# Other fillers in TensorE's program: inside the line of the first products and, new, between the quarter products

## The chip, the cores and the metric

The kernel runs on one core of one Trainium2 chip. The metric is the device time of one execution in microseconds, lower is better; a profiled execution also has a span, from the first to the last instruction that the profile shows.

## The reference

A retention layer (8 batches, 8 heads, 576 positions, head size 64) is followed by a feed-forward layer on the joined heads.

```python
def _attn_ref(q, k, v):
    B, H, S, D_ = q.shape                      # 8, 8, 576, 64
    scores = np.matmul(q, k.transpose(0, 1, 3, 2)) / np.sqrt(D_)
    gamma = 1.0 - 2.0 ** (-5.0 - np.arange(H, dtype=np.float32))
    rel = np.arange(S)[:, None] - np.arange(S)[None, :]
    Dmat = np.where(rel >= 0, gamma[:, None, None] ** rel[None, :, :], 0.0)
    return np.matmul(scores * Dmat[None], v)
# x: (4608, 512), the heads of a token side by side
h = x @ w_in                                   # (512, 2048)
out = (h * np.cos(h)) @ w_out                  # (2048, 512)
```

## The kernel before

The 4608 tokens are cut into nine tiles of 512 (`n` = 0 to 8), and for the attention into 18 blocks of 256, two to a tile. The attention is done in chunks with a running state: `turned` transposes queries and keys, `sums_of` makes the states, `scores` the masked scores, `out_own` and `out_carried` the outputs. All of these are 64x64 matmuls, each on a quarter of the array; the text calls them quarter matmuls. Each takes a weight load and a matmul, so two rows of TensorE's program.

The feed-forward layer of a tile has two parts. `mm1` makes `h` (line 525): from tile 2 on, eight blocks of eight matmuls of 512 columns. ScalarE takes the cosine of a block and VectorE multiplies, and the PSUM bank is then free. The second product is done by `mm2_seven` as seven products of half-size blocks (Strassen's scheme), in the order 1, 2, 6, 4, 7, 5, 3; `product` (line 608) issues each of them as 16 matmuls of 256 columns (line 640). In tiles 3 to 6, product 2 is preceded by transposes, product 4 and product 3 by one `visit` each: a unit of 120 or 128 quarter matmuls that gives one block's outputs and the next block's states and scores. So the order of TensorE's work in such a tile is: 64 matmuls of line 525; product 1; transposes; products 2 and 6; first unit; products 4, 7, 5; second unit; product 3. The order is written out by hand, and every engine runs its program in order.

TensorE's program holds fillers besides. `addr_align(2, k)` puts a row that does nothing where the next row's address, counted in rows, isn't k modulo 2; since weight load and matmul are two rows, calls with k in turn 1, 0, 1, 0 give one row each. In the trace such a row is a NOP of line 508. `spread` (line 500, called at line 533 after each matmul of line 525) puts `fillers[n]` of them evenly between the matmuls of tile n's first product:

```python
    fillers = {0: 96, 1: 80, 2: 80, 3: 126, 4: 48, 5: 64, 6: 64, 7: 128}
```

`product` has none.

Of the kernel before, what the change touches and what calls it, by code (L numbers as in the profile page):

```python
# [17 lines left out]
def kernel(  # L18
# [21 lines left out]
    DG = DM // P  # L40
    ET = DF // P
# [3 lines left out]
    W = 512  # L45
# [44 lines left out]
    w_in_sb = consts.tile([P, DG, DF], BF16)  # L90
    w_out_sb = consts.tile([P, ET, DM], BF16)

    fillers = {0: 96, 1: 80, 2: 80, 3: 126, 4: 48, 5: 64, 6: 64, 7: 128}
    tiles = {}

    class Chunk:
# [400 lines left out]
        for run in rest:  # L497
            run()

    def spread(n, w):  # L500

        want = fillers.get(n, 0)
        done = tiles["g", n, "done"]
        whole = ET * DG * W
        if want and not done:
            nc.tensor.addr_align(2, 0)
        for u in range(done * want // whole, (done + w) * want // whole):
            nc.tensor.addr_align(2, 1 - u % 2)
        tiles["g", n, "done"] = done + w

    def mm1(n, et, c0, w, bank, inside={}):
        if ("g", n) not in tiles:
            tiles["g", n] = gp.tile([P, ET, W], BF16, tag="gT", name="gT")
            tiles["g", n, "done"] = 0
        gT, xT = tiles["g", n], tiles["x", n]
        m = 1024 // w
        ps = psum.tile([P, m, w], F32, tag=bank, name="h")
        steps = [(j, dg) for j in range(m) for dg in range(DG)]
        in_parts = (n, et, c0) in ((0, 0, 0), (0, 4, 0))
        if in_parts:  # L520
            steps.sort(key=lambda u: u[1] // 2)
        for u, (j, dg) in enumerate(steps):
            if u % DG == 0 and u // DG in inside:
                inside[u // DG]()
            nc.tensor.matmul(  # L525
                ps[:, j, :],
                lhsT=w_in_sb[:, dg, (et + j) * P : (et + j + 1) * P],
                rhs=xT[:, dg, c0 : c0 + w],
                start=dg == 0 and not (in_parts and w < 512 and j % 2),
                stop=dg == DG - 1,  # L530
                skip_group_check=in_parts,
            )
            spread(n, w)
        if m in inside:
            inside[m]()

        cosh = cosp.tile([P, m, w], F32, tag="cosh", name="cosh")
        nc.scalar.activation(cosh, ps, ACTF.Sin, bias=half_pi, scale=1.0)  # L538
        nc.vector.tensor_mul(gT[:, et : et + m, c0 : c0 + w], ps, cosh)  # L539
# [3 lines left out]
    def w_quarter(r, c):  # L543
        return w_out_sb[:, r * E2 : (r + 1) * E2, c * N2 : (c + 1) * N2]
# [63 lines left out]
    def product(n, x, early=None):  # L608
        gT = tiles["g", n]
        parts = [(j, 0, N2) for j in range(2)]  # L610
        fold = n in (1, last)
        fresh = x not in ((6, 7, 3) if fold else (6, 7))
        if fresh:
            tag = {1: "n", 2: "st", 4: "m" if n == 1 else "st", 5: "st", 3: "n"}[x]
            if x == 5 and n == last:
                tiles["o", x] = [
                    psum.tile([P, c], F32, tag=t, name="o")
                    for t, c in (("b", N2), ("m", N2 // 2), ("a", N2 // 2))
                ]
            else:  # L620
                ps = psum.tile([P, 2, N2], F32, tag=tag, name="o")
                tiles["o", x] = [ps[:, j] for j in range(2)]
                tiles["all", x] = ps
        if x in (5, 3) and n == last:
            parts = [(0, 0, N2), (1, 0, N2 // 2), (1, N2 // 2, N2)]
        dst = tiles["o", x if fresh else 5 if x == 3 else 1]
        lhs = {1: gT[:, :E2, :256], 2: gT[:, E2:, :256], 4: gT[:, E2:, 256:]}.get(x)
        if lhs is None:
            lhs = tiles["gs", n, x]
        rhs = {1: w_quarter(0, 0), 2: w_quarter(1, 0), 3: w_quarter(1, 1)}.get(x)  # L630
        if rhs is None:
            rhs = w_sum[x]
        order = [(e, i) for e in range(E2) for i in range(len(parts))]
        if len(parts) > 2:
            order.sort(key=lambda u: u[1])
        for u, (e, i) in enumerate(order):
            if early and u == len(order) // 4:
                early()
            j, c0, c1 = parts[i]
            nc.tensor.matmul(  # L640
                dst[i],
                lhsT=lhs[:, e, j * P : (j + 1) * P],
                rhs=rhs[:, e, c0:c1],
                start=(fresh and e == 0 and (i == 0 or len(parts) > 2)),
                stop=(e == E2 - 1 and (i == len(parts) - 1 or len(parts) > 2)),
                skip_group_check=True,
            )
        return parts

    def stored_rows(r0, c0, c1, t, queues=(nc.sync, nc.sync)):  # L650
# [7 lines left out]
    def mm2_seven(n, at, stored, xs=(1, 2, 6, 4, 7, 5, 3), early=None):  # L658
# [26 lines left out]
        for x in xs:  # L685
# [8 lines left out]
            if x == 6 and n > 1:  # L694
                late_sums(n, (3,))
            parts = product(n, x, early)
            if x == 1:
                c11 = copied("a", 1)
# [256 lines left out]
    for n in range(NT):  # L955
# [37 lines left out]
        if n == 0:  # L993
# [24 lines left out]
            order = [(t, e) for e in range(part) for t in range(4)]  # L1018
# [3 lines left out]
            for done, (t, e) in enumerate(order):  # L1022
# [9 lines left out]
                for u in range(2 * (t == 1) if t < 2 else 1) if e == ET - 1 else ():  # L1032
                    u = u if t < 2 else t
# [119 lines left out]
```

## Time and profile before

| what | us |
|---|---|
| median of 3 runs | 293.08 |
| lowest and highest | 292.98 to 293.34 |
| the profiled execution | 292.63 |
| its span | 290.9 |
| line 525, tile 4: 64 matmuls, 48 fillers | 13.81 |
| line 525, tile 7: 64 matmuls, 128 fillers | 13.81 |
| products 4, 7 and 5 of a tile, 48 matmuls | 5.34 |
| a unit of quarter matmuls, tiles 3 to 7 | 1.27 to 1.36 |

The span is what lies between the first and the last instruction; 1.7 us of the profiled execution lie around it. PE is TensorE's matmuls, PEld its weight loads, DVE VectorE, ACT ScalarE, POOL GpSimd, SP SyncE; PEldq marks a row that TensorE's sequencer runs by itself, without the array. A matmul's record lasts longer than the distance to the next, so paces are taken from the distance of starts. The times of the table's last four rows are distances between the start of the first matmul of the part and that of the next part.

### The profile page before, as it was taken

The numbers are of one execution on the slowest core, as the hardware profiler recorded it, in microseconds if no ns is written. First come the engines' busy times: TensorE is split into PE (matmuls) and PEld (weight loads), VectorE is DVE, ScalarE is ACT, GpSimd is POOL, SyncE is SP. The second block draws the span as 40 slices with busy tenths as digits, with TensorE's granted clock in tenths as the row PEclk, the third lists the DMA queues.
The fourth block names the chain that finished last, engine by engine and source line by source line (L and its number), as shares of the span: only waits on it lengthen the run. The fifth ranks groups of instructions, "written<-read, shape, count | busy, mean of one in ns | idle before, by whom it ended". The sixth has DMA issues, their size and how long they took to land.

```text
span 290.9 us, 10529 instructions
## 1 busy us (share of the span) xinstructions
PE 284.3 (98%) x4336; PEld 191.3 (66%) x4336; DVE 218.5 (75%) x309; ACT 170.7 (59%) x200; POOL 147.9 (51%) x169
## 2 busy tenths in 40 slices
PE   7999999999999999999999999999999999999994
PEld 2664446888854786478647874687458845884584
DVE  5767758999967967896789677977698669745943
ACT  6756216756677655676467746673767476536620
POOL 7840435698977993379136923593348024002400
PEclk9999999999999999999999999999999999999999
DMA  7999999997997989837690589139101220122013
GB/s 218 275 171 205 252 235 247 224 220 195 223 224 183 268 207 230 210 78 176 170 227 15 129 200 217 42 99 231 38 0 41 65 49 0 41 51 59 0 38 108
DMA packets 103853, 42.62 MB, mean 146 GB/s; under 512 B 68480, under 2 KB 103296, under 8 KB 103808
## 3 DMA queue, kind: packets, MB, share of 16 engines
q1 hardware_dynamic: 99104, 37.37, 52.5%
q0 software_dynamic: 4256, 4.19, 9.1%
q8 instruction: 36, 0.59, 0.8%
q10 hardware_dynamic: 448, 0.39, 0.4%
q14 instruction: 9, 0.07, 0.1%
HBM read 36.70 MB, written 9.44 MB: 159 GB/s over the span
## 4 chain that ended last, share of the span: by engine, by line
PE 94%; DVE 3%; DMA 1%; issue 0%; ACT 0%; DVEq 0%; ACTq 0%
PE h L525 43%; PE o L640 34%; PE o L1025 5%; PE ov L449 3%; PE tr L239 3%; PE ov L477 2%; PE sc L332 2%; DVE ret L312 1%; PE st L365 1%; DMA fk<-in_k_dram 1%; DVE qks L171 1%; PE sc L299 0%; PE tr L260 0%; ACT ot L670 0%; PE idle L270 0%
## 5 line engine op out<-in xcount | busy, mean ns | idle before, releaser
L525 PE MATMUL h<-xT,w_in_sb 128*128 128x512 bf16 (+1 forms) x656 | 127.4, 353 | 0.0
L539 DVE TENSOR_TENSOR gT<-h,cosh 128x1024 bf16<-128x1024 f32 x72 | 87.8, 1221 | 27.3 <-ACT cosh L538 26.8
L538 ACT ACTIVATE cosh<-h,half_pi 128x1024 f32<-128x1024 f32 x72 | 80.2, 1115 | 40.7 <-PE h L525 40.7
L525 PEld LDWEIGHTS <-w_in_sb 128*128 128x128 bf16 x656 | 63.5, 98 | 58.6 <-DMA w_in_sb<-in_moe_w_in_dram 0.2
L579 POOL TENSOR_TENSOR gs<-gT 128x512 bf16<-128x512 bf16 x30 | 38.1, 1271 | 99.6 <-DVE gT L539 99.0
L640 PEld LDWEIGHTS <-gs 128*128 128x128 bf16 x528 | 49.6, 98 | 5.9
L203 POOL TENSOR_TENSOR qks<-fk,gkc 128x512 bf16<-128x512 f32 x32 | 39.0, 1237 | 5.1 <-DMA fk<-in_k_dram 5.1
L640 PEld LDWEIGHTS <-gT 128*128 128x128 bf16 x384 | 36.6, 98 | 6.1
L666 DVE TENSOR_TENSOR ot<-ot,o 128x512 f32<-128x512 f32 x35 | 23.3, 683 | 20.2 <-ACT ot L670 12.6
L245 ACT COPY qkT<-tr 128x1024 bf16<-128x1024 bf16 x29 | 27.7, 1021 | 12.0 <-PE tr L239 11.0
L203 POOL TENSOR_TENSOR qks<-fq,gq 128x512 bf16<-128x512 f32 x28 | 31.2, 1134 | 4.6 <-DMA fq<-in_q_dram 4.6
L640 PE MATMUL o<-w_out_sb,gs 128*128 128x256 bf16 (+1 forms) x264 | 30.7, 270 | 0.0
L640 PE MATMUL o<-w_out_sb,gT 128*128 128x256 bf16 x256 | 30.6, 273 | 0.0
L640 PE MATMUL o<-ws,gs 128*128 128x256 bf16 (+1 forms) x264 | 30.4, 269 | 0.0
L670 ACT COPY ot<-o 128x512 f32<-128x512 f32 x33 | 19.2, 586 | 18.1 <-PE o L640 17.5
L341 DVE TENSOR_TENSOR ret<-sc,mask_c 128x512 bf16<-128x512 f32 x32 | 20.6, 683 | 7.5 <-PE sc L332 6.6
L214 POOL CAST vb<-fv 128x512 bf16<-128x512 f32 x35 | 22.0, 650 | 6.7 <-DMA fv<-in_v_dram 6.7
L425 ACT CAST sb<-s_all 128x768 bf16<-128x768 f32 (+2 forms) x17 | 15.6, 919 | 14.0 <-DVE s_all L416 13.9
L416 DVE TENSOR_TENSOR s_all<-st,s_all 128x256 f32<-128x256 f32 x49 | 20.7, 422 | 1.9 <-PE st L365 0.6
L496 ACT CAST xT<-ov 128x1024 bf16<-128x1024 f32 x16 | 16.2, 1012 | 9.6 <-PE ov L477 9.4
L579 DVE TENSOR_TENSOR gs<-gT 128x512 bf16<-128x512 bf16 (+1 forms) x24 | 15.8, 660 | 0.6
L579 DVE TENSOR_TENSOR gs<-gs,gT 128x1024 bf16<-128x1024 bf16 x16 | 15.2, 948 | 0.3
(83 smaller groups left out, 213.7 us busy)
## 6 DMA issues: line engine op xcount, KB each, us to landing
out_dram<-ot SPq DMA_DIRECT2D x68, 128.0 KB, 2.7
fk<-in_k_dram SPq DMA_DIRECT2D x28, 256.0 KB, 5.3
fv<-in_v_dram SPq DMA_DIRECT2D x28, 256.0 KB, 4.8
fq<-in_q_dram SPq DMA_DIRECT2D x12, 512.0 KB, 5.0
w_out_sb<-in_moe_w_out_dram POOLq DMA_DIRECT2D x4, 512.0 KB, 9.6
fq<-in_q_dram SPq DMA_DIRECT2D x4, 384.0 KB, 7.3
fk<-in_k_dram SPq DMA_DIRECT2D x2, 512.0 KB, 5.0
fv<-in_v_dram SPq DMA_DIRECT2D x2, 512.0 KB, 5.9
```

The lines of the kernel that those rows point to most:

```text
L203: return eng.tensor_tensor(out=dst.rearrange("p b a d -> p a b d"), in0=src.rearrange("p (a b) d -> p a b d", a=2), in1=by.rearrange("p (a ...
L214: runs[y](vb[:, y], f[:, :, y, :] if j < NP_B else f[:, y])
L245: lambda r=r: evacs[r](tiles["qkT", j][:, :, :, :, r * HP : r * HP + HP], pss[r])
L341: nc.vector.tensor_tensor(out=ret[:, he].rearrange("p b y i -> p (b y) i"), in0=ps[he].rearrange("p b y i -> p (b y) i"), in1=mask_c.unsqu ...
L416: nc.vector.tensor_tensor(out=s32[:, u], in0=ps[c.half][:, c.y], in1=s32[:, u - 1] if u else tiles["run"], op=ALU.add,)
L525: nc.tensor.matmul(ps[:, j, :], lhsT=w_in_sb[:, dg, (et + j) * P : (et + j + 1) * P], rhs=xT[:, dg, c0 : c0 + w], start=dg == 0 and not (i ...
L538: nc.scalar.activation(cosh, ps, ACTF.Sin, bias=half_pi, scale=1.0)
L539: nc.vector.tensor_mul(gT[:, et : et + m, c0 : c0 + w], ps, cosh)
L579: i = eng.tensor_tensor(out=tiles["gs", n, x][:, e : e + step], in0=a[:, e : e + step], in1=b[:, e : e + step], op=op_,)
L640: nc.tensor.matmul(dst[i], lhsT=lhs[:, e, j * P : (j + 1) * P], rhs=rhs[:, e, c0:c1], start=(fresh and e == 0 and (i == 0 or len(parts) > 2)),
L666: return lambda: nc.vector.tensor_tensor(out=out_, in0=in0, in1=in1, op=ALU.add)
L670: held.append(lambda ps=tiles["all", x]: nc.scalar.copy(t, ps))
```

## The change

The numbers of fillers in `mm1` become others for tiles 2 to 7. The padding itself moves into a helper, `filled`, which `product` calls too: after each of the 48 matmuls of products 4, 7 and 5 in tiles 3 to 6 it puts its share of `between[n]` fillers, 160 or 176 to a tile, so three or four to a matmul. The total of fillers goes from 686 to 950 in `mm1`, and from none to 688 in the products. Nothing else is changed.

```diff
-    fillers = {0: 96, 1: 80, 2: 80, 3: 126, 4: 48, 5: 64, 6: 64, 7: 128}
+    fillers = {0: 96, 1: 80, 2: 31, 3: 103, 4: 144, 5: 144, 6: 144, 7: 208}
+    between = {3: 160, 4: 176, 5: 176, 6: 176}
...
-    def spread(n, w):
-
-        want = fillers.get(n, 0)
-        done = tiles["g", n, "done"]
-        whole = ET * DG * W
+    def filled(want, done, w, whole):
+
         if want and not done:
             nc.tensor.addr_align(2, 0)
         for u in range(done * want // whole, (done + w) * want // whole):
             nc.tensor.addr_align(2, 1 - u % 2)
+
+    def spread(n, w):
+
+        done = tiles["g", n, "done"]
+        filled(fillers.get(n, 0), done, w, ET * DG * W)
         tiles["g", n, "done"] = done + w
...
             nc.tensor.matmul(
                 dst[i],
...
                 stop=(e == E2 - 1 and (i == len(parts) - 1 or len(parts) > 2)),
                 skip_group_check=True,
             )
+            if x in (4, 7, 5):
+                filled(between.get(n, 0), (4, 7, 5).index(x) * len(order) + u, 1, 3 * len(order))
         return parts
```

## The prediction

> **What bounds the kernel now.** I read the page first, then what TensorE waits for, then the chain of waits around one tile's products, then the records of the filler line, and last the granted clock in a stretch where TensorE is only partly busy.
>
> ```profile
> PE 284.3 (98%) x4336; PEld 191.3 (66%) x4336; DVE 218.5 (75%) x309; ACT 170.7 (59%) x200; POOL 147.9 (51%) x169
> ...
> q8 instruction: 36, 0.59, 0.8%
> ...
> PE 94%; DVE 3%; DMA 1%; issue 0%; ACT 0%; DVEq 0%; ACTq 0%
> ```
>
> TensorE is busy 98% of the span and is 94% of the chain that ended last. Queue q8 brings 36 packets of 16 KB; the trace has 9369 rows of TensorE's program (4336 weight loads, 4336 matmuls, 685 fillers, 12 others), so one packet is 256 rows of 64 bytes: these are the blocks that the change speaks of. TensorE's own waits, as the waits view gives them:
>
> ```profile
> PE idle L270 <- DVE zeros L814: 1.3, 1, 1.3
> PE ov L449 <- DVE ret L312: 0.5, 2, 0.3
> ```
>
> Both lie at the start. From tile 3 on TensorE waits for nobody, so anything that slows it goes into the end one for one. The chain, in order of time, through tile 3's products (start, length, what):
>
> ```profile
> 132.07 0.25 PE ov L449 x16
> 132.32 0.26 PE st L365 x32
> 132.57 0.29 PE sc L332 x32
> 132.87 0.27 PE ov L449 x15
> 133.13 0.29 PE ov L477 x31
> 133.43 5.34 PE o L640 x48
> 138.77 0.25 PE ov L449 x16
> ```
>
> The five pieces before 133.43 are one stretch of quarter matmuls, 256 rows in 1.36 us; 138.77 begins the next. Between them stand the 48 matmuls of products 4, 7 and 5, in 5.34 us, 111 ns each, and no row of another kind. Here the change puts 160 fillers (tile 3) or 176 (tiles 4, 5, 6).
>
> What does one filler cost? The answers on the filler line for three windows, 231.3 to 235.5 us (products of line 525 in tile 7, two fillers to a matmul), the first two fillers alone in it, and 171.2 to 172.7 us (tile 5, one filler to a matmul):
>
> ```profile
> L508 PEldq NOP  x48: 13/13/13, 231.3 to 235.5; - x48
> L508 PEldq NOP  x2: 13/13/13, 231.3 to 231.4; - x2
> L508 PEldq NOP  x16: 13/13/13, 171.2 to 172.7; - x16
> ```
>
> A filler becomes a NOP whose record lasts 13 ns, but the next record starts far later. Of the 166 pairs of fillers with nothing between them, 145 start 70 or 71 ns apart; with a matmul and its weight load between them the usual distance is 90 or 91 ns. So TensorE's sequencer spends **70 ns on a filler** and about 20 ns on a weight load and matmul. It is the sequencer's own pace and not that of a full queue: in those 4.2 us of tile 7 it passed some 23.5 matmuls, while the array, at 216 ns each, did 19.5. The long windows give more: 4.2 us / 23.5 = 179 ns for two fillers and a matmul, 1.5 us / 15 = 100 ns for one and a matmul, difference 79 ns a filler.
>
> **Why the old fillers are free.** Two fillers and a matmul take the sequencer 2 x 70 + 20 = 160 ns, under the 216 ns of a 512-column matmul: tile 7's block of 64 matmuls with 128 fillers takes 13.81 us, and tile 4's with 48 the same 13.81. The cover is the matmul's length. For a 256-column matmul at 109 to 111 ns it is gone at (111 - 20)/70 = 1.3 fillers.
>
> **The change, part by part.**
>
> Tiles 2 and 3, inside line 525: 80 to 31 and 126 to 103 fillers. Hidden before, hidden after: 0.
>
> Tiles 4, 5 and 6, inside line 525: 144 each, 2.25 to a matmul, 2.25 x 70 + 20 = 178 ns under 216: 0. The cover would be gone at 79 ns x 2.5 fillers. The sequencer also stops there for PSUM banks, as much as 3 us at a time, and would only wait less.
>
> Tile 7, inside line 525: 208, 3.25 to a matmul. 208 x 0.070 + 64 x 0.020 = 15.84 us against 13.81: +2.0 us, no longer covered.
>
> Products 4, 7, 5 of tile 3: 160 x 0.070 + 48 x 0.020 = 12.16 us against 5.34: +6.8 us.
>
> The same of tiles 4, 5, 6: 176 x 0.070 + 48 x 0.020 = 13.28 against 5.34: +7.9 us each, +23.8 us. Sum of the uncovered parts: 2.0 + 6.8 + 23.8 = **+32.7 us**.
>
> The sequencer's lead: it stands some 0.4 us ahead where a new product starts (tile 7's first filler at 231.33 comes after the issue of a matmul that the array starts at 231.72). After a quarter stretch I estimate 0.3 us, which five slowed places give back: -1.5 us.
>
> Block ends: what could be gained? The units of 120 quarter matmuls take 1.27 to 1.31 us in tiles 3 to 7 (tile 3's first, 128 matmuls, 1.36); the fastest of the kernel, in tile 2, 1.16. Bringing all nine down to that is worth 1.2 us and no more. Against it, after product 5 the sequencer arrives with no lead at the second unit, whose last pieces, where the lead is used up, run at 13 to 14 ns a matmul: 120 x 13.5 = 1.6 us for 1.3, four times, another 1.2 us. I set both against each other: 0, with 1.2 us either way.
>
> What queues behind the fillers: on TensorE everything, since its program is read in order; a matmul behind four NOPs can't pass them. VectorE and ScalarE then get their banks later and have more time for each; none of them becomes late by it. The four or so more blocks that q8 must bring are 0.06 MB of 42.6. No DMA, wait or queue of another engine is moved.
>
> Is the slower pace seen by the clock? TensorE's array would work 111 of some 270 ns. The windows view of two stretches near the start (columns: stretch and length, busy time of PE, PEld, DVE, ACT, POOL, granted clock, DMA share, GB/s):
>
> ```profile
> 5.00:9.00 4.00, 3.57 (x38) 1.50 (x36) 3.14 (x9) 2.99 (x7) 2.71 (x6) 1.00 1.15 347
> 9.00:12.50 3.50, 3.14 (x91) 2.12 (x91) 3.50 (x6) 2.24 (x5) 3.38 (x5) 1.00 1.18 320
> ```
>
> The second holds 91 matmuls, some 80 of them quarter ones (8 to 14 ns each elsewhere), about ten of 128 columns (72 ns) and one of 512 (216 ns): 1.6 to 2.1 us of array work in 3.5, about half. The clock stays at 1.00. So 0.
>
> **Sum:** 32.7 - 1.5 = +31.2 us. The profiled execution took 292.63 us, its span of 290.9 and 1.7 around it; 292.63 + 31.2 = 323.8. The median of the runs shown is 0.45 us above that execution, so 324.
>
> Bounds of the filler's price. The nearest rows below: TensorE's EVENT_SEMAPHORE, also run by the sequencer, records 51 ns. At that, 8.16 + 0.96 - 5.34 = 3.8 and 3 x (8.98 + 0.96 - 5.34) = 13.8, tile 7 covered (11.9 under 13.81), +17.6 less 1.2 = 309.5. Above: 79 ns of the long windows gives 8.3 + 3 x 9.5 + 3.9 = 40.7, less 1.5, 332. I take 70, the distance that nearly all neighbouring fillers have; the longer windows hold pauses of other causes. One doubt belongs to the low side: the distances come from an execution that wrote a record of every row. That the profiled execution isn't slower than the others says only that hidden fillers stay hidden.
>
> [...]
>
> **Rivals.** First, **the fillers are nearly free and the change gains.** A filler's record is 13 ns long; if that is its whole price, 176 x 13 + 48 x 20 = 3.2 us hide under 5.34, 208 x 13 + 64 x 20 = 4.0 under 13.81, and what is left is the gain of up to 1.2 us at the block ends: 291.9 us. It decides where a filler costs under 24 ns, (109 - 20)/3.67. For it: the 13 ns, and that 36 blocks are fetched and units differ by up to 0.15 us. Against it: no pair of fillers in the trace starts less than 70 ns apart. Chance 0.08. [...]
>
> Second, **the clock falls too**: the array, idle more than half the time for 12 us, is granted half speed, and what follows runs slowly until it recovers. The ten 512-column matmuls at the very start stand 414 ns apart against 216 later; eight of these after each of the four slowed places lose 8 x 0.2 = 1.6 us, 6.4 in all: 330. Against it the two rows above, for it that no stretch of the trace is as empty for 12 us. Chance 0.06.
>
> Third, **the fillers aren't there**: the call pads only where the row's parity is wrong, so a call could come out empty. Then 293. Against it: 694 calls of the old program gave 685 rows. Chance 0.02.
>
> **Numbers.** The forecast, fillers at 50 to 80 ns with the clock at full, has 0.84; 324 is its value at 70. The range is 308 to 333: the bounds of the price with a little for the block ends, and nearly all of the second rival; left out are the free fillers and prices between 24 and 50 ns. A difference of 0.2%, 0.6 us, is what a measurement of this kernel can tell from no change. Faster 0.06 (most of the first rival), same 0.03 (the rest of it with the third), slower 0.91.
>
> **What would show it.** Products 4, 7 and 5 should take some 12 us in tile 3 and 13 in tiles 4 to 6 in place of 5.34, with L640's matmuls about 270 ns apart and gaps that are put down to issue; tile 7's block of line 525 some 16 us, and tiles 4 to 6's still 13.81. PE's share should fall below 98% if gaps count as idle. About 1638 NOPs, 952 more, and q8 at 40 packets. If products 4, 7, 5 stay near 5.3 us, the price of a filler is wrong and with it all of the forecast; if line 525 slows after the products with a clock under 1.00, the second rival is right.

## The result, and the profile after

The changed kernel takes 336.27 us (median of six runs, 334.68 to 338.92) against 293.17 before: 1.149 times as long, interval 1.146 to 1.152. The forecast was 324 with a range of 308 to 333. The direction was right; of the 43 us the forecast had 31, and the time lies 3.3 us above the range.

The page after: TensorE's line, the granted clock in 40 slices of 8.4 us, the queue that brings the program's blocks, and the engines' shares of the chain.

```profile
PE 317.5 (95%) x4315; PEld 193.1 (58%) x4336; DVE 220.2 (66%) x309; ACT 171.0 (51%) x200; POOL 147.3 (44%) x169
...
PEclk9999999999999999999996999965999599999999
...
q8 instruction: 40, 0.66, 0.8%
...
PE 91%; issue 3%; DVE 3%; DMA 1%; ACT 1%; DVEq 0%; ACTq 0%
```

Two things are new. "issue", time in which TensorE waited for nothing that the profile shows, was 0% and is 3%. And the clock, all nines before, has slices of 6, 6, 5 and 5. (21 matmul records are missing from this trace; the weight loads are complete.) The answer on the filler line for the products of tile 4:

```profile
L506 PEldq NOP  x176: 13/13/13, 172.7 to 186.7; - x176
```

All 176 are there, and the 48 matmuls take 13.97 us with them. The chain of waits from the end of these products through the unit behind them (start, length, what):

```profile
186.13 0.27 PE o L643
186.40 0.04 issue
186.44 0.27 PE o L643
186.71 0.03 issue
186.74 0.32 PE ov L450 x16
187.06 0.26 PE st L366 x32
187.31 0.29 PE sc L333 x32
187.61 0.13 PE ov L450 x15
187.74 0.18 PE ov L478 x17
187.91 1.24 issue
189.15 0.25 PE ov L478 x6
```

Before, line 640 stood in this chain as one piece of 48 matmuls. Now single matmuls stand 0.31 us apart with bits of issue between them, 0.03 and 0.04 us here: before each matmul stand three or four fillers, whose NOPs on the sequencer's row PEldq start at least 70 ns apart. Then, inside the quarter matmuls, six matmuls before the unit ends, TensorE stands for 1.24 us. The waits view shows that this happens in four places, one in each of the tiles 3 to 6 (0.93 to 1.74 us in the timeline):

```profile
PE ov L478 <- issue: 5.1, 4, 1.7
```

The four are not at any place. Counting TensorE's rows in program order (weight load, matmul and filler one each), the stalled rows are 5056, 6336, 7616 and 8896, and divided by 256 (the rows of a block as the prediction counts them; here 40 packets brought 10320 rows) each leaves 192: **they are the first rows of blocks**. A tile's program is 1280 = 5 x 256 rows long here, so equal places in the four tiles leave the same remainder anyway. What shows it is that in the other kernels below, where the stalls of tiles 3 to 6 lie in other parts too, the remainder is again 192 to 194, and that each of these stalls, here and there, ends 1.3 to 1.5 us after a packet of q8 has landed.

The windows view for tile 3's products, and for two stretches that began in the products of tiles 4 and 5 and in tile 5's second unit (columns as in the prediction):

```profile
133.43:146.33 12.90, 11.94 (x56) 4.61 (x49) 3.28 (x7) 3.13 (x4) 5.80 (x8) 1.00 0.67 150
178.69:185.52 6.83, 6.80 (x25) 2.50 (x24) 0.69 (x1) 0.61 (x2) 0.00 (x0) 0.50 0.44 101
226.48:233.31 6.83, 5.88 (x138) 4.39 (x138) 4.28 (x9) 2.25 (x3) 0.00 (x0) 0.50 0.18 43
```

Half speed, 6.83 us each time. There are four such stretches. Three lie within the products, where the matmuls still start some 0.28 us apart (24 weight loads in 6.83 us), as in the 5.91 us at full speed ahead of the first stretch (21 in 5.91); the one at 226.48 covers the second unit of tile 5, product 3 and the first matmuls of tile 6.

So the 43.6 us by which the span grew (334.5 for 290.9) divide as follows, each part measured from the start of its first matmul to the start of the next part:

| part | before | after | us more |
|---|---|---|---|
| products 4, 7, 5, tile 3 | 5.34 | 12.91 | 7.6 |
| the same, tiles 4, 5, 6 | 5.34 each | 13.97 each | 25.9 |
| second units, tiles 3 to 6 | 1.31, 1.30, 1.31, 1.27 | 3.10, 2.59, 2.93, 2.59 | 6.0 |
| line 525, tile 7 | 13.81 | 16.14 | 2.3 |
| product 3 of tile 5 and line 525 of tile 6, half clock | 15.57 | 17.37 | 1.8 |
| sum | | | 43.6 |

### The profile page after: what moved, and what is told of

It is laid out like the page before. It is cut to its first block, busy times and chain, and to the rows that moved or that the text cites. A ratio compares the mean times of both kernels' runs of the same rounds, so it can differ in the third digit from the quotient of the medians.

```text
span 334.5 us, 11462 instructions
## 1 busy us (share of the span) xinstructions
PE 317.5 (95%) x4315; PEld 193.1 (58%) x4336; DVE 220.2 (66%) x309; ACT 171.0 (51%) x200; POOL 147.3 (44%) x169
## 4 chain that ended last, share of the span: by engine, by line
PE 91%; issue 3%; DVE 3%; DMA 1%; ACT 1%; DVEq 0%; ACTq 0%
PE o L643 39%; PE h L528 37%; PE o L1030 4%; PE ov L450 3%; PE tr L240 3%; PE ov L478 2%; PE sc L333 1%; DVE ret L313 1%; PE st L366 1%; DMA fk<-in_k_dram 1%; DVE qks L172 1%; DVE gT L542 0%; PE sc L300 0%; ACT cosh L541 0%; PE tr L261 0%
## 5 line engine op out<-in xcount | busy, mean ns | idle before, releaser
L528 PE MATMUL h<-xT,w_in_sb 128*128 128x512 bf16 (+1 forms) x640 | 128.8, 353 | 1.0 <-issue 0.2
L542 DVE TENSOR_TENSOR gT<-h,cosh 128x1024 bf16<-128x1024 f32 x72 | 87.8, 1222 | 32.5 <-ACT cosh L541 32.2
L643 PEld LDWEIGHTS <-gs 128*128 128x128 bf16 x528 | 50.7, 100 | 28.9 <-issue 17.9
L643 PE MATMUL o<-w_out_sb,gs 128*128 128x256 bf16 (+1 forms) x264 | 42.5, 293 | 0.7
L643 PE MATMUL o<-ws,gs 128*128 128x256 bf16 (+1 forms) x264 | 40.1, 280 | 1.1 <-issue 0.2
L643 PE MATMUL o<-ws,gT 128*128 128x256 bf16 x128 | 24.1, 274 | 1.8
```

Of the source, the lines that this page charges most:

```text
L528: nc.tensor.matmul(ps[:, j, :], lhsT=w_in_sb[:, dg, (et + j) * P : (et + j + 1) * P], rhs=xT[:, dg, c0 : c0 + w], start=dg == 0 and not (i ...
L643: nc.tensor.matmul(dst[i], lhsT=lhs[:, e, j * P : (j + 1) * P], rhs=rhs[:, e, c0:c1], start=(fresh and e == 0 and (i == 0 or len(parts) > 2)),
```

## The experiments

Three questions: what a filler costs in the products, why the second units stall, and when the clock falls. The time in brackets behind a median is that of the kernel before on the same chip.

**Block ends moved by 64 rows.** The changed kernel with fillers added in tile 2, where they are hidden.

```diff
-    fillers = {..., 2: 31, 3: 103, ...}
+    fillers = {..., 2: 95, 3: 103, ...}
```

> The changed kernel with 64 fillers more in tile 2's line 525 (95 for 31, 1.5 to a matmul, hidden), so that every later block end lies 64 rows earlier against the work. In the changed kernel the second units take 2.6 to 3.1 us for 1.3, and stall each time at the row that begins a block. Theory A, the block isn't there yet (it becomes usable some 4.0 to 4.5 us after the sequencer crossed the end before, and only 2.7 us lie between): now the end before lies 94 rows, 4.8 us of fillers, ahead of the unit, the next end 162 rows into it, so no stall; second units 1.3 us each, total 336.3 - 5.5 = about 331. Theory B, the units are slow because the sequencer arrives without a lead and must feed them by itself: nothing changes, 336.

Measured 330.26 us (292.93), 6.0 less than the changed kernel. The timeline of TensorE in tile 3's second unit:

```profile
146.06 0.32 PE L450 MATMUL ov<-ret,vb 64*64 64x64 bf16 x16
146.19 0.44 PE L366 MATMUL st<-vb,qks 64*64 64x64 bf16 x32
146.46 0.47 PE L333 MATMUL sc<-qkT 64*64 64x64 bf16 x32
146.74 0.32 PE L450 MATMUL ov<-ret,vb 64*64 64x64 bf16 x16
146.88 0.41 PE L478 MATMUL ov<-qkT,sb 64*64 64x64 bf16 x24
147.22 0.61 PE L643 MATMUL o<-w_out_sb,gs 128*128 128x256 bf16 x4
```

1.16 us and no stall, where the changed kernel's unit took 3.10, though the same fillers stand ahead of the unit. That is what A, the missing block, had said. B, the prediction's reason for slower units, falls altogether. In tiles 4 to 6 the units took 1.54 to 1.75 us, under half clock and without a stall. So the four units together went from 11.2 to 6.2 us, which is 5.0 of the 6.0 us. The other 1.0 is not the units': the half-speed stretches fell elsewhere, and product 3 of tile 5 with line 525 of tile 6 took 16.39 us for 17.37.

How long a block takes can be read where fillers stand on both sides of the end, since each is timed:

| kernel, tile | sequencer crosses a block's end | next packet starts on q8 | the first row behind the next end runs | from crossing |
|---|---|---|---|---|
| changed, 3 | 144.8 | 146.8 | 149.2 | 4.5 |
| changed, 4 | 185.1 | 186.8 | 189.2 | 4.0 |
| changed, 5 | 225.0 | 226.7 | 229.3 | 4.3 |
| changed, 6 | 267.1 | 268.7 | 271.1 | 4.0 |
| ladder (below), 3 | 141.3 | 142.7 | 145.5 | 4.2 |
| ladder, 4 | 178.2 | 179.5 | 182.1 | 3.9 |
| ladder, 5 | 215.9 | 217.5 | 220.0 | 4.2 |

In these seven places the next packet starts 1.3 to 2.0 us after the crossing, and the first row behind the next end runs 3.9 to 4.5 us after it, 4.2 in the mean. The packet itself takes 1.0 to 1.4 of that, and the first row runs 1.3 to 1.5 us after it has landed, also where it took longer. In the changed kernel 30 rows of fillers and products (1.6 us) and then 226 rows of quarter matmuls (1.1 us) make up one block: 2.7 us, 1.5 short of those 4.2, where TensorE stood for 0.93 to 1.74 us.

**The old kernel with the ends at these places.** No fillers in the products.

```diff
-    fillers = {0: 96, 1: 80, 2: 80, ...}
+    fillers = {0: 96, 1: 120, 2: 146, ...}
```

> The kernel before with 40 fillers more in tile 1 and 66 more in tile 2 (both hidden), so that the block ends lie where the changed kernel has them against the second units of tiles 4 to 6: 30 rows before the unit begins and 14 before it ends. No fillers in the products. If the place of the ends alone makes the stall, 1.3 us or more at each of three second units, total 297 or above. Theory A with a lead: the sequencer crosses the first end some 30 rows earlier against the array, so 60 rows of 256-column matmuls (3.3 us) and 1.0 us of the unit lie between, 4.3 us, about as long as a block needs: stalls of 0 to 0.3 us each, 293 to 294.

Measured 296.69 us (292.93), ratio 1.0128, 1.0108 to 1.0148. The timeline in tile 4's second unit, the idle time in brackets:

```profile
172.12 0.36 PE L477 MATMUL ov<-qkT,sb 64*64 64x64 bf16 x18
173.12 0.25 PE L477 MATMUL ov<-qkT,sb 64*64 64x64 bf16 x6 [0.64 <-issue]
```

The same six matmuls before the unit's end, the same first row of a block. Units of 2.16, 1.99 and 2.26 us in tiles 3 to 5, so 0.7 to 0.95 each, and another stall of this kind in tile 1. My 0 to 0.3 was too low, though each stall is smaller than the 1.3 to 1.8 us by which the changed kernel's units grew; that the sequencer's lead makes the difference no run shows by itself. The place of the ends alone makes one, without any filler in the products.

**Fillers of line 525 alone.**

```diff
-    between = {3: 160, 4: 176, 5: 176, 6: 176}
+    between = {}
```

> The new fillers of line 525 alone, none in the products. The price of 70 to 80 ns a filler: tiles 4 to 6 stay at 13.81 us with 144 fillers, tile 7 takes about 16.1 with 208, products 4, 7, 5 are back at 5.34 us; second unit back at 1.3 us; granted clock 1.00 throughout: 293.2 + 2.3 = 295.5. If instead fillers in line 525 cost the changed kernel more than its tile 7, the total is above 296.5.

Measured 296.78 us (292.93), ratio 1.0132, 1.0107 to 1.0157; a little over the bound that I had named. Products 5.34, clock 1.00, tile 7's line 525 16.23 us: +2.4 as expected. The rest is stalls at the first rows of blocks: the second units of tiles 2 and 5 took 1.78 and 1.97 us, tile 4's line 525 14.01, while tiles 3 and 4 had second units of 1.16. In the profiled execution another 1.2 us lie ahead of tile 2's first unit: 0.5 of it in line 525 of tile 1, at a row that runs 1.15 us after a packet has landed, the rest around 46 us, in part waits for VectorE.

**One filler to a matmul.**

```diff
-    between = {3: 160, 4: 176, 5: 176, 6: 176}
+    between = {3: 48, 4: 48, 5: 48, 6: 48}      # with the old fillers of line 525
```

> The old fillers of line 525 and 48 fillers, one to a matmul, in products 4, 7 and 5 of tiles 3 to 6. If what counts is the sequencer's pace against the array's, 70 + 20 = 90 ns hide under 109 to 111: products at 5.34 to 5.5 us, total 293 to 294.5. Rival: every filler put there adds its 70 ns: 4 x 48 x 0.07 = 13.4 us, 306.5.

Measured 296.30 us (292.93), ratio 1.0116, 1.0096 to 1.0135. The timeline, and the answer on the filler line for tile 4's products:

```profile
165.08 1.92 PE L643 MATMUL o<-ws,gT 128*128 128x256 bf16 x16
166.83 1.91 PE L643 MATMUL o<-w_out_sb,gs 128*128 128x256 bf16 x16
168.58 1.91 PE L643 MATMUL o<-ws,gs 128*128 128x256 bf16 x16
170.42 0.32 PE L450 MATMUL ov<-ret,vb 64*64 64x64 bf16 x16
```
```profile
L506 PEldq NOP  x47: 13/13/13, 165.0 to 169.6; - x47
```

165.08 to 170.42 is 5.34 us, as without fillers: one to a matmul cost nothing here, and not 70 ns each. The 3.4 us are again mostly stalls at first rows of blocks: second units of 1.97, 2.05 and 2.91 us in tiles 2, 4 and 5, product 3 of tile 3 2.18 us for 1.76.

**A ladder of fillers.**

```diff
+    fillers = {..., 4: 176, 5: 192, 6: 64, 7: 128}
+    between = {3: 96, 4: 112, 5: 128, 6: 144}
```

> Steps of fillers: in products 4, 7 and 5 there are 96, 112, 128 and 144 in tiles 3, 4, 5 and 6; in line 525 176 in tile 4 and 192 in tile 5, the old numbers elsewhere. If the sequencer's pace sets the time, the products grow in a straight line with the number: at 70 ns and 20 ns a matmul 7.7, 8.8, 9.9, 11.0 us; by a line through the changed kernel's two values (160: 12.91, 176: 13.97) 8.7, 9.7, 10.8, 11.9. Line 525: 13.8 to 13.9 in tile 4, about 15 in tile 5. If other things than the pace make the changed kernel's price, the line breaks between two and three fillers to a matmul. Clock: 1.00 if it falls only where the array is under some 40 percent busy (144 fillers leave it 45 percent). Total with two or three stalls at block begins 313 to 319.

Measured 318.68 us (292.92). Products 4, 7, 5, with the changed kernel's two values:

| fillers | 48 | 96 | 112 | 128 | 144 | 160 | 176 |
|---|---|---|---|---|---|---|---|
| us | 5.34 | 8.14 | 9.19 | 10.35 | 11.69 | 12.91 | 13.97 |

From 96 on this is nearly a straight line, with the points within 0.13 us of it: (13.97 - 8.14)/80 = 73 ns a filler, and (8.14 - 96 x 0.073)/48 = 24 ns for a matmul with its weight load. These two are averages. Filler by filler, the changed kernel's trace has 684 distances inside the four groups of products: 465 are 70 or 71 ns and 165 are 90 or 91, with a matmul between. The rest are longer. About every 20 rows the sequencer pauses for another 10 to 154 ns, 0.65 us in all in each of the four groups; what it does then no run shows. Line 525 took 14.03 us with 176 fillers and 14.92 with 192; 208 took 16.14 in the changed kernel. The clock stayed at 1.00 in the profiled execution; the other one had a mean of 0.993, which the record does not place. The stalls here are no matter of units: this one lies in product 3, which a block's end had reached.

```profile
179.60 0.94 PE L643 MATMUL o<-w_out_sb,gs 128*128 128x256 bf16 x7
182.09 1.16 PE L643 MATMUL o<-w_out_sb,gs 128*128 128x256 bf16 x9 [1.55 <-issue]
```

**160 fillers in all four tiles**, 16 more in line 525 of tiles 4 to 6 to keep the ends where the first experiment had them.

```diff
-    fillers = {..., 2: 95, 3: 103, 4: 144, 5: 144, 6: 144, 7: 208}
-    between = {3: 160, 4: 176, 5: 176, 6: 176}
+    fillers = {..., 2: 95, 3: 103, 4: 160, 5: 160, 6: 160, 7: 208}
+    between = {3: 160, 4: 160, 5: 160, 6: 160}
```

> The kernel with the ends moved by 64, but 160 fillers instead of 176 in the products of tiles 4 to 6 and the 16 put into line 525 (160 for 144, hidden), so that the block ends lie at the second units as there. Clock theory: the granted clock halves where the products run at 3.67 fillers to a matmul (array 38 percent busy; in both runs so far it fell in tiles 4 to 6) and not at 3.33 (41 percent; it never fell in tile 3). Then no fall here, products 12.9 us each, total 330.3 - 3 x 1.1 - 2.3 of half clock = 324.7. Rival: tile 3 was spared by chance or by what lies before it; the clock falls here too in tiles 4 to 6, 326.5 to 327.5.

Measured 325.07 us (292.92), 5.2 less than with the ends moved alone. The page's clock line, and two of the products in the windows view:

```profile
PEclk9999999999999999999999999999999999999999
```
```profile
171.65:184.53 12.88, 11.83 (x57) 4.55 (x49) 2.86 (x6) 2.91 (x4) 5.89 (x8) 1.00 0.64 153
209.03:221.87 12.84, 11.86 (x57) 4.61 (x49) 2.77 (x6) 2.91 (x4) 5.88 (x8) 1.00 0.65 154
```

The clock does not fall, in none of the four executions, and all four second units take 1.16 us. The array does 48 x 111 ns = 5.34 us in 12.88, 41%; with 176 it was 38%, and the clock fell in all three such tiles of both kernels. More than these two shares the runs do not show. That the products last 1.1 us longer with 176 is not the reason: the clock fell 3.6 to 7.3 us after their start, well before the end of either.

**Can the ends be placed better than before?** Three tries with the kernel before and other fillers in line 525 alone.

```diff
+    fillers = {0: 96, 1: 80, 2: 80, 3: 126, 4: 74, 5: 64, 6: 64, 7: 128}   # later ends
+    fillers = {}                                                            # no fillers
+    fillers = {0: 96, 1: 80, 2: 80}                                         # early only
```

> The kernel before with 26 fillers more in tile 4's line 525, so that the last block end lies 206 rows before the second units of tiles 4 to 6 for 180; no fillers in products. There two other kernels had units of 1.16 us for 1.30. If the place of the end decides that: 3 x 0.14 us less, 292.5, and 292.9 if it doesn't.

> No fillers anywhere. The second units of tiles 3 to 6 then begin 69, 5, 197 and 133 rows behind a block end, the first ones 229, 181, 117 and 53. A block that is used up before the next has come stalls at its end; so far units that began 20 to 68 rows behind an end stalled by 0.6 to 1.8 us, those at 94 and over hardly. Expected 1 to 2 us at tile 4's second unit, up to 1 at tile 3's and at tile 6's first: 294 to 297. If fillers do nothing but fill: 293.

> The old fillers of tiles 0, 1 and 2 alone (256 rows, one block, so that the ends lie at the early work as in the kernel before and at tiles 3 to 7 as in the one without fillers). Without any fillers one stall of 1.25 us at a block's begin in tile 1 was seen, and second units of 1.16 us in tiles 3 to 5 for 1.30. If both hold by themselves, 293.95 - 1.25 = 292.7, and with the three or four quicker units 292.4 at best, a gain of 0.1 to 0.2 percent over the kernel before, no more than can be measured. If the fillers of tiles 3 to 7 are needed for other places, above 293.2.

Later ends: 292.95 us (292.92), ratio 0.9998, 0.9988 to 1.0008. The units didn't follow the place as I thought: 1.27 to 1.34 us in tiles 4 to 6. No fillers: 293.95 us (292.92), ratio 1.0038, 1.0024 to 1.0051, with one stall of 1.25 us between weight loads at the first row of a block in tile 1. Tile 4's second unit, six rows behind an end, took 1.16 us, and not the 1 to 2 us more that I had expected. But it used up its block, and the stall stands at that block's end: product 3 behind it took 2.06 us for 1.76, with a pause at the first row of the next block, 1.48 us after its packet had landed. Early only: 292.91 us (293.03), ratio 0.9992, 0.9979 to 1.0006. That kernel has the same small stall in tile 4 (2.11 us). So all 686 old fillers together are worth 1 us, those of tiles 0 to 2 do it, and no version here beats the kernel before.

## Why the prediction was wrong in size

By its own steps:

- **Fillers in the products**, 12.16 and 13.28 us: right in kind, 12.91 and 13.97 measured, and 2.9 us of the 12.4 that were missing. The prices of 70 and 20 ns were right for neighbours, as the distances in the changed kernel show. What the terms left out are the sequencer's pauses, 0.65 us in each of the four groups. They raise the average to 73 and 24 ns, between the two values that the trace of before offered, 70 from neighbouring fillers and 79 from long windows. The prediction had put the longer windows down to pauses of other causes and dropped them; they come in the products too.
- **Tile 7's line 525**, +2.0: 2.3 measured. Tiles 4 and 5 with 144 fillers stayed at 13.81, as said; the hidden numbers of tiles 2 and 3 too.
- **The sequencer's lead**, -1.5 us: there is next to none to give back in the products. In tiles 4 to 6 the record of their first filler starts only 0.04 to 0.06 us ahead of their first weight load. In tile 7's line 525 it starts 0.48 us ahead, and that lead is in the 2.3 us already.
- **Block ends against lost lead**, set to 0 with 1.2 us either way: this is the step that failed, with the largest part of what was missing. The second units lost 6.0 us. I had looked only for what a block end inside a stretch costs, found 0.15 us at most, and never asked what happens when a stretch uses up a whole block. The change put the ends 30 rows ahead of each unit, just where fillers had also made the sequencer late: 2.7 us of rows lay between the two ends, and the first row behind the second ran 4.0 to 4.5 us after the first was crossed. Moving the ends took all four stalls away: the units were back at 6.2 us for 11.2 with three of them at half clock, and at 4.6 us in the kernel with 160 fillers, at full clock.
- **The clock**, 0, with the rival at 0.06: it did fall, in tiles 4 to 6 but not in tile 3, and cost 1.8 us and not the rival's 6.4, since most of the half-speed time fell on products in which the fillers set the pace anyway, 0.28 us to a matmul at either clock. The row whose array work I had worked out as evidence, about half busy over 3.5 us, was above both shares that the experiments compare: the clock fell at 38% over 14 us and not at 41% over 13 us. (The matmuls of 128 columns in that row stand mostly 55 to 67 ns apart, not 72, which is 0.1 us less of array work.)
- **The rivals of free fillers and absent fillers** are out: the fillers are there, one to a 256-column matmul cost nothing (5.34 us) and two did (8.14).

The corrections are 2.9 + 0.3 + 1.5 + 6.0 + 1.8 = 12.5 us; 31.2 + 12.5 = 43.7, and the span grew by 43.6. The kernel with 160 fillers everywhere has neither such a stall nor a slow clock from tile 3 on and costs 32.2 us over the kernel before; what is left there is nearly all the sequencer's pace. That this is near the forecast's 31 is luck: by the prediction's own terms this kernel, with 48 fillers fewer in the products, would have cost 27.8 (4 x 6.82 and 2.0, less 1.5).

In the kernel before no stall at a block's end is seen from tile 2 on: TensorE's waits there are 1.3 and 0.5 us for VectorE, at the start. The changed kernel's second units took 1.3 to 1.8 us more, 0.93 to 1.74 of it the stall.

## What to carry to other kernels

One filler to a 256-column matmul cost nothing here, and two made 8.14 us of 5.34: count the sequencer's time for everything between two matmuls (70 ns a filler and 20 ns a matmul in these traces) and compare it with the array's for one matmul (111 ns for 256 columns, 216 for 512). When padding is used to place code blocks, look at how long each block lasts, not at whether an end falls inside a busy stretch: the changed kernel's stalls came behind blocks that had lasted 2.7 us, where a row behind the next end ran some 4.2 us after the crossing. A stretch of fast rows that uses up nearly a whole block, like these units with 240 rows in 1.16 to 1.31 us, is where to look first. Where a slow pace empties the array, look at the clock in every stretch before calling it unchanged: here it was halved with the array 38% busy.

## What the runs showed of the hardware

A filler on TensorE recorded 13 ns and, where no matmul covered it, cost 70 to 71, or 73 with the sequencer's pauses spread over all of them. In the seven stalls of the table the first row of a block of 256 rows ran 3.9 to 4.5 us after the sequencer had crossed into the block ahead of it, and 1.3 to 1.5 us after a packet had landed; 256 rows of quarter matmuls took 1.36 us in tile 3 of the kernel before. The clock was halved in stretches of 6.83 us in the changed kernel and 10.24 us in the one with the ends moved (its mean of 0.953 over 328.3 us is what three of these give), in products and in one case right behind them, where the array was 38% busy for 14 us, and not where it was 41% busy for 13 us. What stays open is why a unit of 120 quarter matmuls takes 1.16 us in some places and 1.27 to 1.34 in others where no stall is seen: it does not go by the place of the block ends alone. The longer second units have one gap of 0.1 to 0.2 us between two weight loads, at changing places.
